# Reordering batch 0's attention in a one-core linear-attention and MLP kernel: part of q loaded behind v, one slot of k rotated on GpSimd

## The chip, the cores and the metric

The kernel runs on one core of a Trainium2 chip. The metric is device time in microseconds (us). The kernel before took 292.59 us (median of 3 runs, 292.51 to 292.88); lower is better. A core has a matrix engine (TensorE, PE in the profile), a vector engine (VectorE, DVE), an activation engine (ScalarE, ACT), GpSimd (POOL) and SyncE (SP), which here only issues DMAs. GpSimd issues DMAs too, among them those that cast from f32 to bf16 on the way.

## What is computed

```python
# q, k, v: [8 batches, 8 heads, 576, 64] f32; w_in [512, 2048], w_out [2048, 512]
theta = pi / 2 * arange(576) / 576
phi(x) = concat([relu(x) * cos(theta), relu(x) * sin(theta)], -1)   # 128 features
kv  = einsum('bhsf,bhsd->bhfd', phi(k), v)
z   = phi(k).sum(axis=2)
num = einsum('bhsf,bhfd->bhsd', phi(q), kv)
den = einsum('bhsf,bhf->bhs', phi(q), z)[..., None] + 1e-06
x   = (num / den) as [4608 tokens, 512]
h   = x @ w_in
out = (h * sigmoid(1.702 * h)) @ w_out
```

## The kernel before

Per batch, 512 of the 576 tokens are worked on at once; the other 64 tokens of each batch (the "tails") are collected in `xt` and go through the MLP together at the end. The program is written as straight-line code, and each engine executes its instructions in the order in which the kernel calls them; buffers come from rotating pools, so an instruction that takes a buffer also waits until the buffer's last reader is done. `pmm` has four PSUM buffers (one bank each), `pat` two (named `at` in the profile, two banks each).

Of batch 0, q, k and v are laid out in nine slots `j` of 64 elements per partition; a tile's half of the partitions is one of two heads. The steps, by name:

- `trig` (L135) makes the features of one slot of q or k: two operations (with cos and with sin), on VectorE, on ScalarE (`act=True`) or on GpSimd (`eng=`). For k they land in `kr`, for q in `qn0`.
- `ksum(j)` (L214) sums k's features over the slots on PE; `ksum_evac` (L221) puts the sum into column 64 of `kvs` on VectorE.
- `qturn_pe(c)` (L167) transposes slots 2c and 2c+1 of q's features on PE, and `qevac(c)` (L174) copies them out into `qT`, on VectorE or (`act=True`) on ScalarE.
- `kv_mm` (L202) multiplies features and v on PE, `kv_evac` (L210) copies the result into `kvs` on VectorE, for heads 0 to 3 and 4 to 7 separately in batch 0.
- `den_early(0)` (L241) computes the denominators of the first 128 tokens ahead of the numerators.
- `num_mm(c)` (L226) makes numerators (and denominators) of 128 tokens in an `at` buffer, `num_div(c)` (L248) divides them on VectorE into `xn`.
- `xturn_mm(c)` (L269) transposes `xn` on PE into the same `at` buffer, and `xturn_evac` (L276) copies it into `x` on ScalarE. `xturn_dma` (L282) does both with one transposing DMA on SyncE; the tail takes it.
- `mm1_part(b, fc, t0, t1)` (L291) is the first MLP matmul for one of the 16 column groups `fc` of w_in and some tokens; `mm1(b, fc)` (L303) does all 512 tokens and `gelu(fc)` (L298) on ScalarE. `mm2` (L327) is the second matmul, and at its end evicts on ScalarE and stores.
- `idle(n, w)` (L341) issues n matmuls on a constant tile, which compute nothing that is used.

Loads of batch 0: SyncE issues k in two DMAs (384 and 768 KB) and q in two (512 and 640 KB, L61 to L63). GpSimd waits for k's first part (a one-element copy, L130) and then issues v in two halves (L132, cast to bf16) and w_in pieces 0 and 1 (L133, L134); after its rotation of q's slot 8, it waits for v (L411) and issues w_in 2 and 3, batch 1's k, q and v, and w_out.

The order around the change is written out by hand from L383 on. Batch 0's attention ends in `start_block(0)` (L354), which interleaves `mm1` of the first four column groups, 128 tokens at a time, with the last numerators and x's transposes, and ends with `mm1(0, 4)`; the loop at L447 goes on with `mm1(0, 5)`. Batch 1 calls the same function with `opened=True`, as it does the opening steps itself. Stores of the last batch go through SyncE, those of the other batches through GpSimd (L338). At the program's end SyncE waits once for each of the semaphores that its DMAs use in turn (eight of them) and for the other queues'.

Of the kernel before, what the change touches and what calls it, by code (L numbers as in the profile page):

```python
# [19 lines left out]
def kernel(  # L20
# [9 lines left out]
    nc = tc.nc  # L30
# [24 lines left out]
    def src_of(src, b, i0=0, i1=NI):  # L55
        return src[b, 2 * i0:2 * i1].rearrange("(i hh) (p j) d -> (hh p) i (j d)", hh=2, j=NS)
# [1 line left out]
    qf = one.tile([128, 2560], F32, name="qf")  # L58
    kf, vf, vb = raw("kf"), raw("vf"), raw("vb", BF16)
    qf0 = qf[:, 0:NI * S].rearrange("p (i e) -> p i e", i=NI)  # L60
    for t, src, cut in ((kf, k, 192), (qf0, q, 256)):  # L61
        nc.sync.dma_start(out=t[:, :, 0:cut], in_=src_of(src, 0)[:, :, 0:cut])  # L62
        nc.sync.dma_start(out=t[:, :, cut:S], in_=src_of(src, 0)[:, :, cut:S])  # L63


    NP = NS + 5
# [56 lines left out]
    def load_win(g):  # L123
        nc.gpsimd.dma_start(out=w_in_sb[g], in_=win_r[:, :, ts(g, 512)])
# [5 lines left out]
    nc.gpsimd.tensor_copy(gate[0:1, 0:1], kf[0:1, 0, 0:1])  # L130
    for i in (0, 2):
        nc.gpsimd.dma_start(out=vb[:, i:i + 2], in_=src_of(v, 0, i, i + 2))  # L132
    load_win(0)  # L133
    load_win(1)  # L134
    def trig(dst, src, j, act=False, eng=nc.vector):  # L135
        i = src[:, :, ts(j, 64)]
        for cs, w in enumerate((cosw, sinw)):
            o = dst[:, j, :, ts(cs, 64)]
            if act:
                nc.scalar.activation(o, i, AF.Relu, scale=w[:, j:j + 1])  # L140
            else:
                eng.tensor_scalar(o, i, 0.0, w[:, j:j + 1], op0=MAX, op1=MUL)  # L142
# [24 lines left out]
    def qturn_pe(c, home=None):  # L167
        tp = pmm.tile([128, 2, NI, 128], BF16, name="mm") if home is None else home
        for j in range(2 * c, min(2 * c + 2, NS)):
            for i in range(NI):  # L170
                nc.tensor.transpose(tp[:, j % 2, i], qn0[:, j, i, :], ident)  # L171
        tps[c] = tp

    def qevac(c, act=False):  # L174
        n = min(2 * c + 2, NS) - 2 * c
        o = qT[:, :, ds(c * 128, n * 64)].rearrange("f h (j p) -> f j h p", j=n)
        i = tps.pop(c)[:, 0:n].rearrange("f j i (hh p) -> f j (i hh) p", hh=2)
        if act:
            nc.scalar.activation(o, i, AF.Copy)
        else:  # L180
            nc.vector.tensor_copy(o, i)

    def at_homes():
        t = pat.tile([128, 2, 512], F32, name="at")
        return [t[:, u].bitcast(BF16).rearrange("p (j i f) -> p j i f", j=2, i=NI) for u in range(2)]
# [24 lines left out]
    def kv_evac(i0, i1, n=65):  # L210
        o = st["kvs"][:, :, i0:i1, 0:n]
        nc.vector.tensor_copy(o, st["ps", i0].rearrange("p hh (i e) -> p hh i e", e=65)[:, :, :, 0:n])  # L212
# [13 lines left out]
    def num_mm(c):  # L226
        ps = pat.tile([128, 2, 512], F32, name="at")
        for h in range(H):
            i, hh = divmod(h, 2)
            nc.tensor.matmul(ps[:, h // 4, ds((h % 4) * 65, 65)], qT[:, h, ts(c, 128)],  # L230
                             st["kvs"][:, hh, i, 0:65], start=True, stop=True)
        nums[c] = [ps]
# [8 lines left out]
    def den_early(c):  # L241
        d = pmm.tile([128, 2, 4], F32, name="mm")
        for h in range(H):
            nc.tensor.matmul(d[:, h // 4, h % 4:h % 4 + 1], qT[:, h, ts(c, 128)],
                             st["kvs"][:, h % 2, h // 2, 64:65], start=True, stop=True)
        return inv_of(d)

    def num_div(c, inv=None):  # L248
        ps = nums[c][0]
        pv = ps[:, :, 0:260].rearrange("p a (h e) -> p a h e", h=4)  # L250
        if inv is None:
            inv = inv_of(pv[:, :, :, 64])
# [10 lines left out]
    def x_open(b):  # L263
        x[b] = xpool.tile([128, KC, MT], BF16, name="xT")
# [4 lines left out]
    def xturn_mm(c):  # L269
        ps, xn = nums[c]  # L270
        xv = xn.rearrange("p a h e -> p (a h e)")
        for kc in range(KC):
            o = ps[:, kc // 2, ds(264 + (kc % 2) * 64, 64)].bitcast(BF16)
            nc.tensor.transpose(o, xv[:, ts(kc, 128)], ident)  # L274

    def xturn_evac(b, c):  # L276
        ps = nums.pop(c)[0]
        i = ps[:, :, 264:392].bitcast(BF16).rearrange("p a (k t) -> p a k t", k=2)
        o = x_of(b, c).rearrange("p (a k) t -> p a k t", a=2)
        nc.scalar.activation(o, i, AF.Copy)  # L280
# [10 lines left out]
    def mm1_part(b, fc, t0, t1):  # L291
        if t0 == 0:
            hp[fc] = pmm.tile([128, MT], F32, name="mm")
        for kc in range(KC):
            nc.tensor.matmul(hp[fc][:, t0:t1], w_in_of(kc, fc), x[b][:, kc, t0:t1],  # L295
                             start=(kc == 0), stop=(kc == KC - 1))

    def gelu(fc):  # L298
        g = gpool.tile([128, MT], BF16, name="g")
        nc.scalar.activation(g, hp.pop(fc), AF.Gelu_apprx_sigmoid)  # L300
        gT[fc] = g
# [25 lines left out]
    def mm2(b, t, lo, hi, c0=0, c1=d_model):  # L327
        if lo == 0:
            yp[t, c0] = pmm.tile([128, d_model], F32, name="mm")
        for fc in range(lo, hi):  # L330
            w = gT[fc][:, ts(t, 128)] if t < 4 else gl_t[:, fc, ts(t - 4, 128)]
            nc.tensor.matmul(yp[t, c0][:, c0:c1], w, w_out_sb[:, fc, c0:c1],  # L332
                             start=(fc == 0), stop=(fc == FC - 1))
        if hi == FC:
            ysb = ypool.tile([128, d_model], F32, name="ysb")
            nc.scalar.activation(ysb[:, c0:c1], yp[t, c0][:, c0:c1], AF.Identity)  # L336
            for p0, n, dst in rows(b, t):
                eng = nc.sync if b == B - 1 else nc.gpsimd  # L338
                eng.dma_start(out=dst[:, c0:c1], in_=ysb[p0:p0 + n, c0:c1])  # L339

    def idle(n, w=None):  # L341
        if w is None:
            w = pmm.tile([128, 512], F32, name="mm")
        for _ in range(n):
            nc.tensor.matmul(w, warm[:, 0:128], warm, start=True, stop=True)  # L345
        return w
# [4 lines left out]
    def vt_rhs(r, i, j):  # L351
        return vt[r, j, i, 0:65]

    def start_block(b, opened=False):  # L354

        if not opened:
            xturn_mm(0)
            xturn_evac(b, 0)
            num_mm(2)
            num_div(2)  # L360
            xturn_mm(1)
            xturn_evac(b, 1)
        def part(c, *fcs):
            for fc in fcs:
                mm1_part(b, fc, c * 128, c * 128 + 128)

        for c in range(2):
            part(c, 0, 1, 2, 3)
            num_mm(c + 3)
            num_div(c + 3)  # L370
            xturn_mm(c + 2)
            xturn_evac(b, c + 2)
        xturn_dma(b, 4)
        part(2, 0, 1, 2)
        part(3, 0, 1)
        part(2, 3)
        part(3, 2, 3)
        for fc in range(4):
            gelu(fc)
        mm1(b, 4)  # L380
# [2 lines left out]
    w = idle(12)  # L383
    for j in (0, 1):
        trig(kr, kf, j)
    for j in (2, 6, 7, 8):
        trig(kr, kf, j, act=True)
    for j in (3, 4, 5):
        trig(kr, kf, j)
    kv_open(0, 2)  # L390
    kv_open(2, 4)
    for j in (0, 1, 2):
        ksum(j)
    for j in (3, 6, 4, 7, 5):
        idle(1, w)
        ksum(j)
    idle(1, w)
    ksum(8)
    for j in (0, 1):
        trig(qn0, qf0, j)  # L400
    ksum_evac()
    idle(1, w)
    qturn_pe(0)
    for j in (2, 3):
        trig(qn0, qf0, j, act=True)
    idle(2, w)
    qturn_pe(1)
    for j in (4, 5):
        trig(qn0, qf0, j)
    trig(qn0, qf0, 8, eng=nc.gpsimd)  # L410
    nc.gpsimd.tensor_copy(gate[0:1, 1:2], vb[0:1, 3, 0:1])  # L411
    load_win(2)
    load_win(3)
    kv_mm(0, 2, vb_rhs, 0, 64)
    qturn_pe(2)
    for j in (6, 7):
        trig(qn0, qf0, j, act=True)
    qevac(0)
    qevac(1)
    qevac(2, act=True)  # L420
    inv0 = den_early(0)
    kv_evac(0, 2, 64)
    kv_mm(2, 4, vb_rhs, 0, 64)
    kv_evac(2, 4, 64)
    qturn_pe(3)
    qevac(3, act=True)
    num_mm(0)
    num_div(0, inv0)
    num_mm(1)
    num_div(1)  # L430
    qturn_pe(4)
    qevac(4)
    idle(2)
    x_open(0)
    start_block(0)


    load(kf, k, 1)
# [57 lines left out]
    num_mm(2)  # L496
    num_div(2)
    mm2(0, 3, 12, 16)
    start_block(1, opened=True)


    for b in range(1, B):
# [73 lines left out]
```

## Time and profile before

| what | us |
|---|---|
| median of 3 runs | 292.59 |
| the profiled execution | 292.54 |
| its span, from the first to the last instruction | 290.8 |
| PE busy | 284.3 (98%) |
| VectorE busy | 124.0 (43%) |
| ScalarE busy | 132.9 (46%) |
| GpSimd busy | 35.9 (12%) |
| mean DMA rate | 180 GB/s |

The page gives for each engine its busy time, then the chain of work that ended last, followed back from the last instruction, with the share of the span of each engine. A timeline row has the start in us, the duration, the engine, the line and the operation, output and inputs with their shapes, and, in brackets, how long the engine had been idle before it and what released it. A group's row has busy time and mean duration in ns. PE's matmuls are pipelined: a 128-column matmul takes 0.22 us, but the next can begin 0.0555 us later. "PEld" is the load of weights ahead of a matmul.

### The profile page before, as it was taken

The numbers are of one execution on the slowest core, as the hardware profiler recorded it, in microseconds if no ns is written. First come the engines' busy times: TensorE is split into PE (matmuls) and PEld (weight loads), VectorE is DVE, ScalarE is ACT, GpSimd is POOL, SyncE is SP. The second block draws the span as 40 slices with busy tenths as digits, with TensorE's granted clock in tenths as the row PEclk, the third lists the DMA queues.
The fourth block names the chain that finished last, engine by engine and source line by source line (L and its number), as shares of the span: only waits on it lengthen the run. The fifth ranks groups of instructions, "written<-read, shape, count | busy, mean of one in ns | idle before, by whom it ended". The sixth has DMA issues, their size and how long they took to land.

```text
span 290.8 us, 5790 instructions
## 1 busy us (share of the span) xinstructions
PE 284.3 (98%) x2331; PEld 155.1 (53%) x2331; DVE 124.0 (43%) x356; ACT 132.9 (46%) x232; POOL 35.9 (12%) x68
## 2 busy tenths in 40 slices
PE   6999999999999999999999999999999999999995
PEld 2785466755555555555455545554555455544444
DVE  4964544933648363826482568156725200000000
ACT  7957654692156214630463136412651167651111
POOL 6650044101210001001100110011000100000000
PEclk9999999999999999999999999999999999999999
DMA  7999999683679858975798479846974400002322
GB/s 250 244 212 290 371 287 367 165 192 104 134 242 288 209 137 292 244 191 145 247 269 218 129 196 319 219 108 182 359 84 79 112 36 3 0 0 57 85 77 72
DMA packets 67866, 52.48 MB, mean 180 GB/s; under 512 B 47968, under 2 KB 57952, under 8 KB 67840
## 3 DMA queue, kind: packets, MB, share of 16 engines
q1 hardware_dynamic: 60560, 32.91, 46.0%
q0 software_dynamic: 7280, 19.21, 22.9%
q8 instruction: 18, 0.29, 0.4%
q14 instruction: 8, 0.07, 0.1%
HBM read 36.70 MB, written 9.44 MB: 159 GB/s over the span
## 4 chain that ended last, share of the span: by engine, by line
PE 96%; DMA 2%; ACT 0%; DVE 0%; SPq 0%; issue 0%; ACTq 0%
PE mm L332 43%; PE mm L295 38%; PE mm L312 5%; PE at L230 3%; PE at L207 3%; DMA kf<-in_k_dram 2%; PE mm L171 1%; PE mm L345 1%; PE at L171 1%; PE at L274 1%; DVE kr L142 0%; PE mm L218 0%; ACT xT L280 0%; SPq L62 0%; ACT ysb L336 0%
## 5 line engine op out<-in xcount | busy, mean ns | idle before, releaser
L332 PE MATMUL mm<-w_out_sb,g 128*128 128x512 bf16 (+1 forms) x528 | 117.9, 373 | 0.0
L295 PE MATMUL mm<-xT,w_in 128*128 128x512 bf16 (+1 forms) x608 | 113.2, 345 | 0.0
L300 ACT ACTIVATE g<-mm 128x512 bf16<-128x512 f32 x128 | 75.2, 599 | 30.2 <-PE mm L295 30.0
L295 PEld LDWEIGHTS <-w_in 128*128 128x128 bf16 x608 | 61.8, 113 | 49.5
L332 PEld LDWEIGHTS <-g 128*128 128x128 bf16 x528 | 48.7, 98 | 49.5
L336 ACT ACTIVATE ysb<-mm 128x512 f32<-128x512 f32 (+1 forms) x37 | 21.7, 586 | 109.7 <-PE mm L332 106.7
L339 POOL DMA_DIRECT2D out_dram<-ysb x36 | 19.4, 540 | 172.9 <-ACT ysb L336 171.1
L142 DVE TENSOR_SCALAR kr<-kf,cosw 128x256 bf16<-128x256 f32 x64 | 22.8, 357 | 30.7 <-DMA kf<-in_k_dram 30.7
L254 DVE TENSOR_TENSOR xn<-at,inv 128x512 bf16<-128x512 f32 x40 | 27.6, 691 | 1.7 <-PE at L230 0.4
L142 DVE TENSOR_SCALAR kr<-kf,sinw 128x256 bf16<-128x256 f32 x64 | 22.1, 345 | 0.0
L236 DVE TENSOR_SCALAR den<-at 128x8 f32<-128x8 f32 x39 | 6.5, 166 | 33.1 <-PE at L230 33.1
L230 PEld LDWEIGHTS <-qT 128*128 128x128 bf16 x320 | 14.6, 97 | 8.1 <-issue 0.8
L212 DVE CAST kvs<-at 128x520 bf16<-128x520 f32 (+1 forms) x9 | 5.6, 635 | 29.6 <-PE at L207 29.6
L230 PE MATMUL at<-kvs,qT 128*128 128x65 bf16 x320 | 15.9, 193 | 0.7 <-ACT xT L280 0.7
L155 DVE TENSOR_SCALAR qn<-qf,sinw 128x512 bf16<-128x512 f32 (+1 forms) x30 | 14.4, 479 | 0.0
L155 DVE TENSOR_SCALAR qn<-qf,cosw 128x512 bf16<-128x512 f32 (+1 forms) x30 | 14.3, 476 | 0.0
L312 PE MATMUL mm<-xt,w_in 128*128 128x512 bf16 x64 | 14.0, 379 | 0.0
L332 PE MATMUL mm<-w_out_sb,gl_t 128*128 128x512 bf16 x64 | 14.0, 379 | 0.0
L313 ACT ACTIVATE gl_t<-mm 128x512 bf16<-128x512 f32 x16 | 9.6, 597 | 4.2 <-PE mm L312 4.2
L312 PEld LDWEIGHTS <-w_in 128*128 128x128 bf16 x64 | 7.2, 113 | 6.6
L207 PEld LDWEIGHTS <-kr 64*128 64x128 bf16 x576 | 9.3, 94 | 2.7 <-issue 2.5
L332 PEld LDWEIGHTS <-gl_t 128*128 128x128 bf16 x64 | 6.2, 98 | 7.6
(63 smaller groups left out, 115.9 us busy)
## 6 DMA issues: line engine op xcount, KB each, us to landing
kf<-in_k_dram SPq DMA_DIRECT2D x5, 1152.0 KB, 6.8
vf<-in_v_dram SPq DMA_DIRECT2D x5, 1152.0 KB, 9.6
qf<-in_q_dram SPq DMA_DIRECT2D x5, 1024.0 KB, 6.0
out_dram<-ysb POOLq DMA_DIRECT2D x20, 256.0 KB, 2.7
kf<-in_k_dram POOLq DMA_DIRECT2D x2, 1152.0 KB, 11.3
vf<-in_v_dram POOLq DMA_DIRECT2D x2, 1152.0 KB, 16.4
w_in<-in_moe_w_in_dram POOLq DMA_DIRECT2D x4, 512.0 KB, 9.3
w_out_sb<-in_moe_w_out_dram POOLq DMA_DIRECT2D x4, 512.0 KB, 18.7
```

What stands on the lines that cost most here:

```text
L142: eng.tensor_scalar(o, i, 0.0, w[:, j:j + 1], op0=MAX, op1=MUL)
L155: nc.vector.tensor_scalar(o, i, 0.0, sc, op0=MAX, op1=MUL)
L207: nc.tensor.matmul(st["kv", i][:, hh, ds(col, n)], kr[r, j, i, :], rhs(r, i, j), start=(j == 0), stop=(j == NS - 1))
L230: nc.tensor.matmul(ps[:, h // 4, ds((h % 4) * 65, 65)], qT[:, h, ts(c, 128)], st["kvs"][:, hh, i, 0:65], start=True, stop=True)
L254: nc.vector.tensor_tensor(xn, pv[:, :, :, 0:64], inv.unsqueeze(3).to_broadcast([128, 2, 4, 64]), op=MUL)
L295: nc.tensor.matmul(hp[fc][:, t0:t1], w_in_of(kc, fc), x[b][:, kc, t0:t1], start=(kc == 0), stop=(kc == KC - 1))
L300: nc.scalar.activation(g, hp.pop(fc), AF.Gelu_apprx_sigmoid)
L312: nc.tensor.matmul(hps, w_in_of(kc, fc), xt[:, kc, :], start=(kc == 0), stop=(kc == KC - 1))
L313: nc.scalar.activation(gl_t[:, fc, :], hps, AF.Gelu_apprx_sigmoid)
L332: nc.tensor.matmul(yp[t, c0][:, c0:c1], w, w_out_sb[:, fc, c0:c1], start=(fc == 0), stop=(fc == FC - 1))
L336: nc.scalar.activation(ysb[:, c0:c1], yp[t, c0][:, c0:c1], AF.Identity)
L339: eng.dma_start(out=dst[:, c0:c1], in_=ysb[p0:p0 + n, c0:c1])
```

## The change

Loads: q's slots 0 to 5 come in one DMA from SyncE behind k, and slots 6 to 8 in one DMA from GpSimd behind v. The four w_in pieces are issued together on GpSimd, behind the rotation of k's slot 8, which moves there from ScalarE; the wait of L411 is gone.

Order: batch 0's steps are interleaved anew. q's slot 4 moves to ScalarE and slots 6 and 7 are rotated later there; the eviction of `qturn_pe(1)` goes from VectorE to ScalarE and that of `qturn_pe(2)` from ScalarE to VectorE; `qturn_pe(3)` is put behind `xturn_mm(0)`, and `qturn_pe(4)`, `num_mm(4)` and the tail's DMA around `mm1(0, 4)`. Of the fillers, three stand ahead of `ksum(8)` instead of one, and five others are gone. `start_block` is left to batch 1, where it turns and evicts x's last 128 tokens ahead of `num_mm(4)` instead of behind it. In the last batch the two stores of the first tail tile go through GpSimd instead of SyncE.

```diff
-    for t, src, cut in ((kf, k, 192), (qf0, q, 256)):
-        nc.sync.dma_start(out=t[:, :, 0:cut], in_=src_of(src, 0)[:, :, 0:cut])
-        nc.sync.dma_start(out=t[:, :, cut:S], in_=src_of(src, 0)[:, :, cut:S])
+    for t, src, c0, c1 in ((kf, k, 0, 192), (kf, k, 192, S), (qf0, q, 0, 384)):
+        nc.sync.dma_start(out=t[:, :, c0:c1], in_=src_of(src, 0)[:, :, c0:c1])
...
     for i in (0, 2):
         nc.gpsimd.dma_start(out=vb[:, i:i + 2], in_=src_of(v, 0, i, i + 2))
-    load_win(0)
-    load_win(1)
+    nc.gpsimd.dma_start(out=qf0[:, :, 384:S], in_=src_of(q, 0)[:, :, 384:S])
...
-                eng = nc.sync if b == B - 1 else nc.gpsimd
+                last = b == B - 1 and t != 4
+                eng = nc.sync if last else nc.gpsimd
...
-    def start_block(b, opened=False):
...
-        for c in range(2):
-            part(c, 0, 1, 2, 3)
-            num_mm(c + 3)
-            num_div(c + 3)
-            xturn_mm(c + 2)
-            xturn_evac(b, c + 2)
+    def start_block(b):
+        part(b, 0, 0, 1, 2, 3)
+        num_mm(3)
+        num_div(3)
+        xturn_mm(2)
+        xturn_evac(b, 2)
+        part(b, 1, 0, 1, 2, 3)
+        xturn_mm(3)
+        xturn_evac(b, 3)
+        num_mm(4)
+        num_div(4)
         xturn_dma(b, 4)
...
-    for j in (2, 6, 7, 8):
+    for j in (2, 6, 7):
         trig(kr, kf, j, act=True)
     for j in (3, 4, 5):
         trig(kr, kf, j)
+    trig(kr, kf, 8, eng=nc.gpsimd)
+    for g in range(4):
+        load_win(g)
...
-    idle(1, w)
+    idle(3, w)
     ksum(8)
     for j in (0, 1):
         trig(qn0, qf0, j)
     ksum_evac()
-    idle(1, w)
     qturn_pe(0)
-    for j in (2, 3):
+    for j in (2, 3, 4):
         trig(qn0, qf0, j, act=True)
-    idle(2, w)
     qturn_pe(1)
-    for j in (4, 5):
-        trig(qn0, qf0, j)
-    trig(qn0, qf0, 8, eng=nc.gpsimd)
-    nc.gpsimd.tensor_copy(gate[0:1, 1:2], vb[0:1, 3, 0:1])
-    load_win(2)
-    load_win(3)
+    qevac(0)
+    trig(qn0, qf0, 5)
     kv_mm(0, 2, vb_rhs, 0, 64)
-    qturn_pe(2)
-    for j in (6, 7):
-        trig(qn0, qf0, j, act=True)
-    qevac(0)
-    qevac(1)
-    qevac(2, act=True)
     inv0 = den_early(0)
+    qevac(1, act=True)
     kv_evac(0, 2, 64)
     kv_mm(2, 4, vb_rhs, 0, 64)
     kv_evac(2, 4, 64)
-    qturn_pe(3)
-    qevac(3, act=True)
+    qturn_pe(2)
+    trig(qn0, qf0, 8, eng=nc.gpsimd)
+    for j in (7, 6):
+        trig(qn0, qf0, j, act=True)
     num_mm(0)
     num_div(0, inv0)
     num_mm(1)
+    qevac(2)
     num_div(1)
-    qturn_pe(4)
-    qevac(4)
-    idle(2)
     x_open(0)
-    start_block(0)
+    xturn_mm(0)
+    xturn_evac(0, 0)
+    qturn_pe(3)
+    qevac(3, act=True)
+    num_mm(2)
+    num_div(2)
+    part(0, 0, 0, 1)
+    xturn_mm(1)
+    xturn_evac(0, 1)
+    part(0, 0, 2, 3)
+    num_mm(3)
+    num_div(3)
+    xturn_mm(2)
+    xturn_evac(0, 2)
+    part(0, 1, 0, 1, 2, 3)
+    part(0, 2, 0)
+    xturn_mm(3)
+    xturn_evac(0, 3)
+    part(0, 2, 1, 2, 3)
+    part(0, 3, 0, 1, 2, 3)
+    for fc in range(4):
+        gelu(fc)
+    qturn_pe(4, at_homes()[0])
+    qevac(4)
+    mm1(0, 4)
+    num_mm(4)
+    num_div(4)
+    xturn_dma(0, 4)
```

Here `part(b, c, *fcs)` calls `mm1_part` for 128 tokens `c` and the column groups `fcs`.

More of the change, by code (lines that the diff above doesn't have):

```diff
@@ L352, in vt_rhs, with part @@
         return vt[r, j, i, 0:65]
-    def start_block(b, opened=False):
[L356 to L365, printed above, removed]
-        for c in range(2):
-            part(c, 0, 1, 2, 3)
-            num_mm(c + 3)
-            num_div(c + 3)
-            xturn_mm(c + 2)
-            xturn_evac(b, c + 2)
+    def part(b, c, *fcs):
+        for fc in fcs:
+            mm1_part(b, fc, c * 128, c * 128 + 128)
+    def start_block(b):
[9 more added lines that the diff above has]
+        num_div(4)
         xturn_dma(b, 4)
[L374 to L377, printed above, removed]
+        part(b, 2, 0, 1, 2)
+        part(b, 3, 0, 1)
+        part(b, 2, 3)
+        part(b, 3, 2, 3)
         for fc in range(4):
@@ L429 @@
     num_mm(1)
+    qevac(2)
     num_div(1)
-    qturn_pe(4)
+    x_open(0)
+    xturn_mm(0)
[21 more added lines that the diff above has]
+    qturn_pe(4, at_homes()[0])
     qevac(4)
-    idle(2)
-    x_open(0)
-    start_block(0)
+    mm1(0, 4)
+    num_mm(4)
+    num_div(4)
+    xturn_dma(0, 4)
     load(kf, k, 1)
@@ L498 @@
     mm2(0, 3, 12, 16)
-    start_block(1, opened=True)
+    start_block(1)
     for b in range(1, B):
```

## The prediction

> **What bounds the kernel.** I read the page's chain of work first, then the busy time by stage, the same chain between 4 and 22 us, the timeline of all engines up to 25 us and the end of SyncE's row.
>
> ```profile
> PE 96%; DMA 2%; ACT 0%; DVE 0%; SPq 0%; issue 0%; ACTq 0%
> ```
>
> TensorE is the chain. The stages show where it is not full (columns: stretch, its length, then PE's busy time and the other engines'):
>
> ```profile
> 4.00:16.00 12.00, 10.37 (x201) 7.33 (x200) 10.23 (x30) 9.26 (x20) 9.41 (x14) 1.00 1.17 278
> 16.00:21.61 5.61, 5.59 (x96) 5.08 (x94) 3.19 (x9) 3.35 (x7) 2.35 (x4) 1.00 1.25 211
> 21.61:287.30 265.69, 265.57 (x2033) 141.60 (x2031) 109.67 (x310) 116.75 (x202) 22.62 (x40) 1.00 0.67 178
> 287.30:290.80 3.50, 0.00 (x0) 0.00 (x0) 0.00 (x0) 0.38 (x1) 0.00 (x0) 1.00 0.11 37
> ```
>
> From 21.61 to 287.30 PE is busy 265.57 of 265.69 us. So a change of batch 0 is worth exactly the shift of the instant at which `mm1(0, 5)` can begin (21.61 us before), and beyond that only the 3.5 us behind PE can give. Batch 0's chain joins PE's dense run here (start, length, what):
>
> ```profile
> 14.89 0.02 issue
> 14.91 0.60 ACT xT L280
> 15.52 0.04 issue
> 15.56 0.40 PE at L230 x8
> 15.96 0.22 PE at L274 x4
> 16.18 0.89 PE mm L295 x16
> ```
>
> From 15.56 PE never stands: 64 `mm1` matmuls of 128 columns (0.0555 us apart, 3.55 us), three `num_mm` and three turns of x (1.6 us with their hand-overs) reach `mm1(0, 4)` at 20.75, which takes 0.86. Ahead of 15.56 are fillers and waits. Can the new order start sooner and stay dense?
>
> **1. The loads.** All four w_in pieces and v share one stream: k's second part (768 KB) landed at 6.24, q's first 512 KB at 7.65, v's halves at 10.73 and 12.15, w_in 0 and 1 at 14.75 and 17.83. At the 386 to 395 GB/s that the stretches from 3 to 8 us show, 384 KB of q moved behind v are worth 1.0 us: q's first six slots land at about 8.3 (768 KB behind k), v at 9.7 and 11.15, q's rest at 12.15. **w_in 0 stays at 14.75**, since the bytes ahead of it are the same. In `mm1` nothing can begin before; that is the floor. The other end: v's first packet came 4.1 us after its issue (at 8.47), while SyncE's loads were still being served. If that is a fixed delay and not the queue ahead, v does not move up with the bytes, and the stream stands idle: v at 10.3 and 11.75, q's rest at 12.85, w_in 0 at 15.4. I take the first, because GpSimd's later stores, with little in the queue, had their first packet 1.1 us after issue. w_in is now issued after the rotation of k (9.15 to 12.3 instead of 5.99); with 1.1 us it is there before the stream, at 12.15, needs it. Batch 1's k is issued on GpSimd at about 14.6 (13.87 before) and reached by the stream at 23, so that costs nothing; of w_out the tightest piece landed at 39.57 and was used at 39.96, and with the late stream (40.2) PE comes as late (40.3).
>
> **2. k's slot 8 on GpSimd.** It costs two of these (the two POOL rows), and leaves ScalarE 0.8 us earlier:
>
> ```profile
> 9.88 1.20 POOL L142 TENSOR_SCALAR qn<-qf,cosw 128x256 bf16<-128x256 f32 x1 [2.37 <-DMA qf<-in_q_dram]
> 9.97 0.66 PEld L171 LDWEIGHTS <-qn 128*128 128x128 bf16 x8
> 9.99 0.57 DVE L142 TENSOR_SCALAR qn<-qf,sinw 128x256 bf16<-128x256 f32 x1
> ...
> 10.48 0.34 DVE L142 TENSOR_SCALAR qn<-qf,cosw 128x256 bf16<-128x256 f32 x1
> ...
> 11.09 1.14 POOL L142 TENSOR_SCALAR qn<-qf,sinw 128x256 bf16<-128x256 f32 x1
> ```
>
> GpSimd is free at 6.77 (its third issue then ends), so k's slot 8 is done at 6.80 + 2.34 = 9.15. PE meets `ksum(8)` behind `ksum(5)` (0.22 later than before, see below) and three fillers of 0.213, at 9.42; so 0.25 us are to spare. Behind `ksum(8)` on PE stand all of q's turns, and on VectorE `ksum_evac`: from about 9.7 on, each us that GpSimd is late is a us on everything.
>
> The reader should see the price to VectorE too: its operation took 0.57 beside GpSimd's start and 0.34 wholly inside GpSimd's 1.20 us. The same 0.2 us were lost at 4.81, 6.26 and 7.07, beside GpSimd's load issues. I charge 0.2 once for each further GpSimd instruction that meets a rotation on VectorE: k's slot 5 ends at 8.63 (8.41 before), q's slot 1 and slot 5 lose 0.2 each.
>
> The Trainium skill, "SBUF — State Buffer", section "Who interferes with whom", speaks against this edit: of a VectorE operation in a two-port mode and a GpSimd one, "Whoever issues first gets the shared pair for the whole instruction; the other **fully blocks** (not throttle)." The operation at 10.48 disagrees, as it ran inside GpSimd's; what the rule would give is the slower rival below.
>
> **3. VectorE's chain** (steps at the rows' pitch: rotation 0.265, q's eviction 0.59, kv's 0.30, division 0.69; 0.04 to 0.05 for each hand-over). Rotations of q 0 and 1 end at 9.88, `ksum_evac` at 9.99; `qturn_pe(0)` ends at 10.32; first eviction of q 10.35 to 11.02, **0.8 earlier** than 11.15 to 11.82. Slot 5 to 11.75, `inv0` to 12.06, kv's evictions to 12.66 (13.36 before; their matmuls start at 10.60 and 11.42, behind v). First division 13.03 to 13.72, **0.70 earlier**. Now comes what was put in between: the eviction of `qturn_pe(2)`, formerly ScalarE's, takes 0.6 on VectorE, so the second division is 14.66 to 15.35, only **0.11 earlier** than 14.77 to 15.46.
>
> **4. PE's run.** `xturn_mm(0)` at 13.76, its eviction 14.18 to 14.77 (ScalarE rotates q's slots 7 and 6 from 12.18 to 13.87, just in time), `qturn_pe(3)` and `num_mm(2)` beside it, first `mm1` part at 15.06 instead of 16.02. What PE has left from there: 64 matmuls of 0.0555 (3.55), three turns and `qturn_pe(4)` (0.89), two `num_mm` (0.49), `mm1(0, 4)` (0.86): 5.8 us. And three waits: `num_mm(3)` takes the second of the two `at` buffers, which the eviction of `xturn_mm(1)` frees at 16.51, behind `qevac(3)` (1.02) on ScalarE: 0.39. `part(3)` waits 0.17 for the last x, `xturn_mm(3)` 0.03. Sum 15.06 + 5.79 + 0.59 = 21.44. The same walk over the kernel before ends at 21.48 where the trace has 21.61, so 0.13 goes on top: 21.57. **Front: -0.05 us.** The early start is spent: `qturn_pe(3)`, `qturn_pe(4)` and the waits now lie inside the run that was dense before. Bounds: without the collisions VectorE is 0.3 earlier and w_in 0 is the floor, -0.31; with the late stream +0.34. The fillers taken out leave PE gaps of at most 0.4 us; after gaps of 0.95 and 0.69 (at 7.20 and 15.56) its granted clock stayed at 1.00, so I charge nothing.
>
> **5. Block 1** gets `start_block`'s new order too. Before, `num_mm(4)` (0.24) filled the time until the third division ended at 52.16, and later PE stood 0.18 at 53.29 for the last x. Now it stands 0.27 at once for that division, and not later: +0.06.
>
> **6. The stores.** Two tails' issues go to GpSimd, which is idle at 263 us, at nothing (cover gone: 0.54 each). The first tail's transposing DMA leaves SyncE at about 22.8 instead of 19.91; the next on that queue came at 53.5 and `mm1_tails` at 245, so it too is free. But one SyncE load and two stores fewer move the last store by three of the eight semaphores that SyncE's DMAs use in turn, from number 2 to number 7. At the end SyncE asks for them in the order 0 to 7:
>
> ```profile
> L571 SPq EVENT_SEMAPHORE  x6: 27/28/28, 289.6 to 289.9; - x6
> ```
>
> These six are the one for the last store (landed 289.62) and five behind it, 0.06 us apart. In the changed program's order the last store's is the last asked for, and the others pass while it is in flight: **-0.30 us**. If they did not, 0.
>
> **Sum.** The profiled execution took 292.54 (span 290.8 and 1.7 around it), the median is 292.59: 292.54 - 0.05 + 0.06 - 0.30 = 292.25.
>
> **Rivals.** A measurement tells about 0.2%, 0.58 us, from no change: below 292.0 is faster, above 293.2 slower.
> - *Forecast, 0.60*: the gain in front is given back; 291.95 to 292.65 with the late stream.
> - *VectorE runs free, 0.20*: no further collisions, and w_in 0, the floor, up to 0.3 early; front -0.3 to -0.6, so 291.7 to 292.0. For it: stores issued on GpSimd later (108.9 us) cost VectorE nothing. Against: every load issue in front did.
> - *w_in comes late, 0.08*: 4.1 us after the issue at 9.15 as v did, so the stream stands from 12.15 to 13.3 and w_in 0 lands at 15.9: front +0.8, 293.05. Against: nothing of SyncE's is queued then.
> - *GpSimd stands behind VectorE, 0.09, slower*: k's slot 8 starts only when VectorE's run over k ends (8.41), is done at 10.75, and `ksum(8)` holds PE, `ksum_evac` and the first eviction of q by 1.1 us: 293.4. It decides from 9.7 us on. For it: VectorE's six operations are back to back there; against: GpSimd started at 9.88 amid four of them.
> - *The end does not shorten, 0.03*: 292.55.
>
> **Range** 291.7 to 293.0: the third rival and both bounds of the loads are nearly in it, the fourth is left out. Faster 0.21 (the second, and the first's low end), within 0.2% 0.70, slower 0.09.
>
> **What would show it.** Right: q's first eviction near 10.4, first division near 13.0 but the second near 14.7; first `mm1` part near 15.1; a wait of PE for ScalarE's xT of 0.3 to 0.4 near 16.5; `mm1(0, 5)` near 21.5; one SyncE wait behind the last landing. Wrong: k's slot 8 ending past 9.7 us, w_in 0 landing past 15.2, or `mm1(0, 5)` before 21.2.

## The result, and the profile after

The changed kernel took 293.55 us (median of 10 runs, 293.07 to 294.29) beside 292.69 for the kernel before (median of 10): a ratio of 1.0028, 95% interval 1.0019 to 1.0037. It is slower, and outside the range of 291.7 to 293.0. The profiled execution took 293.35 us (span 291.65), 0.81 more than that of before.

The stages of the changed kernel, cut at the first `mm1` part, at `mm1(0, 5)` and behind PE's last matmul (stretch, its length, then PE's busy time and the other engines'):

```profile
4.00:15.81 11.81, 10.59 (x190) 6.73 (x189) 10.10 (x27) 8.74 (x20) 10.66 (x13) 1.00 1.14 273
15.81:22.79 6.98, 6.37 (x107) 5.58 (x103) 2.75 (x8) 4.31 (x8) 4.10 (x7) 1.00 1.23 230
22.79:288.50 265.71, 265.50 (x2038) 141.51 (x2034) 110.58 (x313) 116.51 (x201) 24.30 (x42) 1.00 0.67 177
```

PE is still full from `mm1(0, 5)` on, so the time is again the shift of that instant and the end: 22.79 instead of 21.61 is +1.18; from there to the start of PE's last matmul it took 265.35 (265.34 before); and from that start to the end of the span 3.50 instead of 3.88, -0.38. The sum is +0.81. The whole loss arises ahead of 22.79 us, where the forecast had 21.57.

The chain of waits of the changed kernel in that stretch (start, length, what):

```profile
6.20 2.91 DVE kr L140 x6
9.11 1.35 DVE qn L140 x4
10.46 0.04 issue
10.51 0.84 PE mm L169 x12
11.35 0.64 PE at L205 x36
...
13.75 0.70 DVE xn L252
...
17.34 0.37 PE at L228 x7
17.71 0.36 issue
18.07 0.19 PE at L228
```

Two things are to be seen. The chain runs through VectorE's rotations of k, which last 2.91 us for six (2.15 before, 6.26 to 8.41), and reaches the first division at 13.75: the forecast had 13.03, the kernel before 13.73. And in the middle of `num_mm(3)`, between its seventh and its eighth matmul, PE stands 0.36 us for "issue", that is for nothing that the profile shows as a releaser. From start to start the eighth matmul comes 0.55 behind the seventh instead of 0.03, so all that follows is 0.52 later.

VectorE's and GpSimd's rows of the changed kernel, in its timeline, show why k took so long:

```profile
6.90 1.19 POOL L140 TENSOR_SCALAR kr<-kf,cosw 128x256 bf16<-128x256 f32 x1
6.95 0.75 DVE L140 TENSOR_SCALAR kr<-kf,cosw 128x256 bf16<-128x256 f32 x1
7.63 0.62 DVE L140 TENSOR_SCALAR kr<-kf,sinw 128x256 bf16<-128x256 f32 x1
8.04 1.30 POOL L140 TENSOR_SCALAR kr<-kf,sinw 128x256 bf16<-128x256 f32 x1
8.17 0.68 DVE L140 TENSOR_SCALAR kr<-kf,cosw 128x256 bf16<-128x256 f32 x1
8.77 0.33 DVE L140 TENSOR_SCALAR kr<-kf,sinw 128x256 bf16<-128x256 f32 x1
```

Of the four VectorE operations that start inside one of GpSimd's, three take 0.62 to 0.75 us instead of 0.34; the fourth, at 8.77, takes 0.33.

The loads are late too. Of v's two DMAs in the changed kernel (issue, then issue to landing):

```profile
L131 POOL DMA_DIRECT2D vb<-in_v_dram x2: 763/842/922, 4.4 to 5.4; - x2
DMA to landing us min/median/max: 6.2/6.5/6.7
```

That is 10.64 and 12.07 us, 0.09 and 0.08 earlier than before for 384 KB fewer ahead of it; the forecast had 9.7 and 11.15. q's first six slots landed at 8.77 (forecast 8.3), its last three at 13.06 (12.15), w_in 0 at 15.66 (14.75). Neither v (12.07) nor w_in 0 is what the chain above waits for, but the second product with v starts at 12.21, only 0.14 behind its landing.

The stores did what was said. SyncE's waits of the changed kernel at the end, from 289.0 us on and then from 290.5 on:

```profile
L585 SPq EVENT_SEMAPHORE  x9: 27/28/28, 289.3 to 290.7; - x9
...
L585 SPq EVENT_SEMAPHORE  x1: 28/28/28, 290.7 to 290.7; - x1
```

The last landing is at 290.73, and one wait stands behind it instead of six.

### The profile page after: what moved, and what is told of

Its sections match the earlier page's. It is cut to its first block, busy times and chain, and to the rows that moved or that the text cites. A ratio compares the mean times of both kernels' runs of the same rounds, so it can differ in the third digit from the quotient of the medians.

```text
span 291.6 us, 5781 instructions
## 1 busy us (share of the span) xinstructions
PE 285.2 (98%) x2328; PEld 154.9 (53%) x2328; DVE 124.4 (43%) x354; ACT 133.1 (46%) x232; POOL 40.6 (14%) x72
## 4 chain that ended last, share of the span: by engine, by line
PE 94%; DVE 2%; DMA 2%; ACT 1%; issue 0%; SPq 0%; ACTq 0%
PE mm L330 43%; PE mm L293 38%; PE mm L310 5%; PE at L228 3%; PE at L205 3%; DMA kf<-in_k_dram 2%; DVE kr L140 1%; PE at L169 1%; PE at L272 1%; DVE xn L252 0%; PE mm L169 0%; DVE qn L140 0%; ACT xT L278 0%; SPq L62 0%; ACT ysb L334 0%
## 5 line engine op out<-in xcount | busy, mean ns | idle before, releaser
L338 POOL DMA_DIRECT2D out_dram<-ysb x38 | 20.7, 547 | 203.1 <-ACT ysb L334 202.7
L140 DVE TENSOR_SCALAR kr<-kf,sinw 128x256 bf16<-128x256 f32 x64 | 22.7, 355 | 0.0
```

## The experiments

All times in one table. The runs were made on different chips; each ratio is to runs of the kernel before made beside it, whose medians lie between 292.51 and 292.69, so 0.2 us between the medians of two rows says nothing. "k" is the end of VectorE's rotations of k, "v" v's two landings, "division" the start of the first division; `mm1(0, 5)` is, where its first record is missing, the start of `mm1(0, 4)` plus 1.10 (new order) or 0.86 (old), as the complete records show. Landings and starts are those of the profiled execution.

| kernel | median us | ratio to before, 95% | k | v | division | first mm1 | mm1(0, 5) |
|---|---|---|---|---|---|---|---|
| before | 292.69 | | 8.41 | 10.73, 12.15 | 13.73 | 16.02 | 21.61 |
| after | 293.55 | 1.0028 (1.0019 to 1.0037) | 9.11 | 10.64, 12.07 | 13.75 | 15.81 | 22.79 |
| e1 small fillers | 293.14 | 1.0031 (1.0014 to 1.0049) | 9.09 | 10.46, 11.92 | 13.73 | 15.80 | 22.27 |
| e2 k's slot 8 on ScalarE | 293.13 | 1.0024 (1.0009 to 1.0040) | 8.34 | 11.77, 13.19 | 14.77 | 16.84 | 23.28 |
| e3 q on SyncE | 292.79 | 1.0003 (0.9995 to 1.0012) | 8.42 | 10.80, 12.20 | 13.79 | 15.85 | 22.30 |
| e4 both | 293.39 | 1.0026 (1.0013 to 1.0039) | 8.55 | 11.22, 12.62 | 14.20 | 16.27 | 22.71 |
| e5 before, stores | 292.12 | 0.9982 (0.9973 to 0.9990) | 8.27 | 10.69, 12.10 | 13.69 | 15.98 | 21.56 |
| e7 v issued early | 293.68 | 1.0033 (1.0020 to 1.0047) | 8.37 | 9.72, 11.10 | 14.53 | 16.60 | 23.04 |
| e8 q's turn earlier | 293.22 | 1.0024 (1.0013 to 1.0035) | 8.41 | 10.62, 12.00 | 13.62 | 16.34 | 22.78 |
| e9 before, k on GpSimd | 292.57 | 0.9999 (0.9989 to 1.0009) | 8.48 | 11.21, 12.58 | 14.18 | 16.47 | 22.05 |
| e10 q late on SyncE | 294.20 | 1.0048 (1.0020 to 1.0076) | 8.44 | 10.43, 11.89 | 13.47 | 17.16 | 23.60 |
| e11 the same, k on ScalarE | 299.01 | 1.0204 (1.0184 to 1.0224) | 8.70 | 9.66, 11.08 | 13.29 | 21.14 | 28.21 |
| e12 new order, less v | 292.55 | 0.9990 (0.9978 to 1.0003) | 8.45 | 10.06, 10.87 | 13.14 | 15.21 | 21.66 |
| e13 old order, less v | 292.04 | 0.9969 (0.9957 to 0.9981) | 8.50 | 10.22, 11.01 | 13.73 | 16.02 | 21.60 |
| e14 old order, no fillers | 292.15 | 0.9989 (0.9977 to 1.0001) | 8.31 | 10.70, 12.10 | 13.68 | 15.97 | 21.56 |
| e15 the same, less v | 291.93 | 0.9973 (0.9963 to 0.9983) | 8.15 | 9.96, 10.75 | 13.50 | 15.79 | 21.37 |

**The stores alone.** e5 is the kernel before with this edit (a third tail store moves too, so that the last store takes semaphore no. 7):

```diff
-                eng = nc.sync if b == B - 1 else nc.gpsimd
+                last = b == B - 1 and t != 4 and not (t == 5 and p0 == 0)
+                eng = nc.sync if last else nc.gpsimd
```

> The kernel before with the last batch's first three tail stores on GpSimd, nothing else: the last store then has the last of the eight semaphores, as in the changed kernel. By the prediction's step 6 one SyncE wait follows the last landing instead of six, five times 0.06 us: 0.30 us faster, 292.4 beside 292.7. The rival: the end is the last landing and the barrier whatever the order, no difference.

It took 292.12 us against 292.51 of its own runs of before, and in its profile too one SyncE wait stands behind the last landing. So the stores are worth about 0.4 us (0.3 to 0.8 by the ratio's interval), and everything else in the change cost 1.25 (profiled executions, 293.35 against 292.10).

**The pause in `num_mm(3)`.** The fillers at the start of PE's program are made 48 of 128 columns instead of 12 of 512, so that PE's instructions are fetched at other times against its work; nothing else is changed.

```diff
-    w = idle(12)
+    w = pmm.tile([128, 512], F32, name="mm")
+    for _ in range(48):
+        nc.tensor.matmul(w[:, 0:128], warm[:, 0:128], warm[:, 0:128], start=True, stop=True)
```

> The changed kernel with its first twelve fillers of 512 columns cut into forty-eight of 128 columns: the same time on the array, 36 matmuls and weight loads more ahead of all work. The pause of 0.36 us of PE in the middle of num_mm(3) (17.71 to 18.07, the profile names no cause) comes while a 16 KB packet of the instruction queue, begun at 15.83, is under way; before, such a packet began at 14.35 and PE stood from 14.88 to 15.56 anyway. Theory code: PE ran out of instructions; with 36 more ahead the fetch comes over 1 us earlier in the work, the pause goes, and the time falls by 0.3 to 0.5, to about 293.1. Theories GpSimd and loads: the pause belongs to the operands or to the loads, it stays, and the time stays at 293.5.

The front is the same as in the changed kernel until 17.3 us (first division 13.73, first part 15.80), but `num_mm(3)` runs through. The timeline of e1:

```profile
17.34 0.40 PE L228 MATMUL at<-kvs,qT 128*128 128x65 bf16 x8 [0.24 <-ACT xT L278]
17.58 0.39 PE L272 MATMUL at<-ident,xn 128*128 128x128 bf16 x4
```

`mm1(0, 4)` starts 0.51 earlier than in the changed kernel (21.17 against 21.68), and the profiled execution takes 0.49 less (292.86 against 293.35). The medians don't show the gain: beside its own runs of before e1 is 0.63 slower and the changed kernel 0.86, and their ratios can't be told apart. In the records, a packet of 16 KB on the instruction queue begins at 15.83 in the changed kernel, 2.2 us ahead of the eighth matmul of `num_mm(3)`; in e1 it begins at 11.34. In before it came at 14.35 and ran while PE stood anyway for `xT` (14.88 to 15.56). In r1 and r2, two more executions of the changed kernel (below), the pause is at the same matmul (0.21 and 0.32). Here and in these two that matmul, 0.03 behind the seventh, would have come 1.7 to 2.0 us behind the start of the packet, and started 2.2 to 2.5 behind it. In e2, e3, e4, e7 and e8, with the fillers unchanged, it comes 2.6 to 3.2 us behind such a start, and PE does not stand. This fits PE running out of instructions: the new order has the place where it runs out in its dense run, with a few tenths of a microsecond deciding. The records do not name the engine that a packet is for; that it is PE's is argued from these times.

**GpSimd beside VectorE, and q's queue.** e2 puts k's slot 8 back on ScalarE; e3 puts q's last slots back on SyncE; e4 does both; e9 puts k's slot 8 on GpSimd in the old order of e5, with w_in 0 and 1 issued behind it.

```diff
# e2
-    for j in (2, 6, 7):
+    for j in (2, 6, 7, 8):
         trig(kr, kf, j, act=True)
...
-    trig(kr, kf, 8, eng=nc.gpsimd)
# e3
-    for t, src, c0, c1 in ((kf, k, 0, 192), (kf, k, 192, S), (qf0, q, 0, 384)):
+    for t, src, c0, c1 in ((kf, k, 0, 192), (kf, k, 192, S), (qf0, q, 0, 384),
+                           (qf0, q, 384, S)):
...
-    nc.gpsimd.dma_start(out=qf0[:, :, 384:S], in_=src_of(q, 0)[:, :, 384:S])
```

> The changed kernel with k's slot 8 rotated on ScalarE again; all else as changed, so w_in is issued on GpSimd from 6.9 on instead of 9.31. Theory GpSimd: VectorE's rotations of k no longer stretch (0.57 to 0.75 us each in the changed kernel, 0.34 alone), k's slot 5 ends at 8.4 to 8.6 instead of 9.11, q's slots 0 and 1 at about 9.7 instead of 10.45; the gain is 0.5 or more, 293.0. Theory loads: v still lands at 10.6 and 12.1 and holds the second kv matmuls at 12.2, so the first division stays near 13.7 and the gain is at most 0.15 unless w_in 0 lands earlier than 15.66.

> The changed kernel with q's slots 6 to 8 loaded by SyncE behind its slots 0 to 5, ahead of v, as before; one more tail store goes to GpSimd so that the last store keeps its place among the semaphores. Theory loads: q's rest lands near 9.8 instead of 13.06, ScalarE's rotation of slots 7 and 6 and GpSimd's of slot 8 no longer stand behind it, and w_in 0 lands near 14.8 to 15.2; v stays at 10.7 and 12.1 since it did not move up in the changed kernel either; gain 0.3 or more, 293.2. Theory GpSimd: VectorE is as stretched as in the changed kernel, first division near 13.7, gain under 0.15.

> Both moves of the front are undone (k's slot 8 on ScalarE, q's last slots on SyncE behind its first six); the new order and the stores stay (a third tail store goes to GpSimd too, so that the last store keeps its semaphore). Theory (the new order itself costs time, about 0.6 us behind the kernel before with the same stores, which took 292.12; GpSimd's rotation is covered, since v lands last): 292.7 to 293.0 as e3 (292.79), first mm1 near 15.9, mm1(0, 5) near 22.5. Rival (GpSimd's rotation of k and the load on its queue are the price of the change): both are gone, so 292.1 to 292.3 and mm1(0, 5) at 21.6 to 21.9.

> The kernel before with three tail stores on GpSimd, as in e5 (292.12), and with k's slot 8 rotated on GpSimd ahead of the issues of w_in 0 and 1; nothing else is changed. Theory (v lands last, and covers what GpSimd's rotation and its collisions with VectorE cost): k's rotations on VectorE end within 0.5 us of 8.3, v's products start with v's landing, and the time is 292.0 to 292.4. Rival (the rotation on GpSimd costs on the path): ksum(8) or the first eviction of q is 0.5 or more later, mm1(0, 5) with it, 292.6 to 293.2.

In e2 VectorE's rotations of k end at 8.34, so the stretch comes from GpSimd's rotation and not from its DMA issues. (Its profiled execution, 294.17, is a late one beside the median of 293.13: v landed at 13.19 and binds.) But e3 keeps that rotation, and they end at 8.42. The timeline of e3:

```profile
6.34 1.19 POOL L140 TENSOR_SCALAR kr<-kf,cosw 128x256 bf16<-128x256 f32 x1 [0.25 <-DMA kf<-in_k_dram]
6.45 0.57 DVE L140 TENSOR_SCALAR kr<-kf,sinw 128x256 bf16<-128x256 f32 x1
6.93 0.34 DVE L140 TENSOR_SCALAR kr<-kf,cosw 128x256 bf16<-128x256 f32 x1
7.20 0.49 DVE L140 TENSOR_SCALAR kr<-kf,sinw 128x256 bf16<-128x256 f32 x1
```

The same work on both engines, begun 0.56 us earlier on GpSimd since it has no third load to issue: the operations beside its first one take 0.57, 0.34 and 0.49, and VectorE's six take 2.25 us instead of 2.91. This goes through all kernels that rotate k on GpSimd: where that starts at 6.28 to 6.40 (e3, e7, e8, e9, e10), VectorE's k ends at 8.37 to 8.48; where it starts at 6.79 to 6.94, behind the third issue (the changed kernel three times, e1), at 9.01 to 9.15. What in the phase decides it isn't settled.

Yet e3's first division is at 13.79, no earlier. The chain of e3, ahead of the second product with v:

```profile
5.33 6.87 DMA vb<-in_v_dram
12.20 0.04 issue
12.24 0.71 PE at L205 x36
```

With VectorE free, v binds at the same instant (12.24; 12.21 in the changed kernel). The two stand in parallel, so undoing one shows nothing in front. What e3 gains in its profiled execution, 0.46 us (292.89 against 293.35), is the pause, which it does not have: from the first part to `mm1(0, 5)` it takes 6.45 instead of 6.98. e4 should have been as fast as e3 and was 0.6 slower: v landed at 12.62 and binds, and PE stood 0.26 up to 43.28 for an eviction of batch 1's q. e9 was 0.45 slower than e5, not 0.0 to 0.3: v landed at 12.58, and its late first product (11.26) waits in its chain for v's first landing (11.21), not for the rotation. r3 below shows such landings without any rotation on GpSimd, so the price of the rotation in the old order stays open between 0 and 0.45.

**An earlier v, and one step of the order.** e7 drops the copy that holds GpSimd until k's first part is there, so v is issued at 2.3 us; e8 is e3 with `qturn_pe(3)` and its eviction ahead of `xturn_mm(0)`.

```diff
# e7
-    nc.gpsimd.tensor_copy(gate[0:1, 0:1], kf[0:1, 0, 0:1])
# e8
-    xturn_mm(0)
-    xturn_evac(0, 0)
     qturn_pe(3)
     qevac(3, act=True)
+    xturn_mm(0)
+    xturn_evac(0, 0)
```

> The changed kernel without the one-element copy that holds v's issue on GpSimd until k's first part has landed: v is issued at about 2.3 us instead of 4.4. Theory (v's landing is set by the queues ahead of it and by the engines that it finds busy, not by the bytes that SyncE has left): v's first packets come 1 to 2 us earlier and v lands at 9.0 to 10.2 and 10.5 to 11.7; the first division then starts at 13.1 to 13.4 instead of 13.75, and the time is 292.9 to 293.2. Rival (the bytes share one stream): k and q land later by what v gains, 0.5 to 1.5 us, VectorE's rotations follow them, and the time is 293.4 to 294.0.

> e3 (q's last slots on SyncE) with one step of the order moved: the transpose of q's slots 6 and 7 and its eviction on ScalarE come ahead of the first transpose of x instead of behind it. Theory (ScalarE's eviction of q, 1.02 us ahead of the second eviction of x, holds num_mm(3) and every later part): the second eviction of x ends 0.3 to 0.6 earlier than 17.32, mm1(0, 5) starts 0.2 to 0.4 earlier than 22.52, 292.4 to 292.6. Rival (the eviction only changes its place on ScalarE, and the first x comes later by as much): first mm1 at 16.2 to 16.8, time 292.8 to 293.3.

In e7 v lands at 9.72 and 11.10, as its theory had it, but q's first slots at 9.54 (8.77 in the changed kernel); the chain goes through them, and the division comes at 14.53. For the time (293.68) that is the rival: the bytes share one stream. e8 is its rival too: the first x is 0.5 later (first `mm1` part 16.34), and nothing comes back.

**Why v landed late.** e10 issues q's last slots on SyncE behind q's first ones' landing, so nothing of q stands behind v in GpSimd's queue, and has the small fillers; e11 also takes GpSimd's rotation of k away. r1 and r2 are the changed kernel again, r3 and r4 are e5 again, each one execution.

```diff
-    nc.gpsimd.dma_start(out=qf0[:, :, 384:S], in_=src_of(q, 0)[:, :, 384:S])
...
+    nc.scalar.activation(qf0[0:1, 0, 384:385], qf0[0:1, 0, 0:1], AF.Copy)
+    nc.sync.dma_start(out=qf0[:, :, 384:S], in_=src_of(q, 0)[:, :, 384:S])
```

> The changed kernel with two things taken away: q's last slots leave GpSimd's queue (SyncE issues them when q's first six slots have landed, near 8.8 us, so that v still has the stream first), and the instruction fetch pause (the 12 fillers of 512 columns are 48 of 128, as in e1). A third tail store goes through GpSimd, so that the last store keeps its semaphore. Theory (v's bytes did move up, but one late DMA engine holds each landing, and such engines come with a second load behind v in GpSimd's queue): v's last packet ends near 10.9 and v lands at 9.7 to 10.0 and 11.2 to 11.4; first division 13.1 to 13.6, mm1(0, 5) at 21.6 to 22.0, time 292.2 to 292.6, with a narrow spread of the runs. Rival (late engines come whatever queue follows): v lands after 10.4 and 11.7, time 292.9 to 293.3.

> e10 with k's slot 8 on ScalarE again, so GpSimd rotates nothing beside VectorE. Theory (with v early, VectorE's collisions with GpSimd, 1.0 us up to q's slot 1, are the next thing on the path): k's rotations end near 8.4, first eviction of q near 10.4, first division 0.2 to 0.4 before e10's, time 0.2 to 0.4 below e10's. Rival (v still binds): the same time as e10 within 0.2.

> The changed kernel once more, for a second look at its loads. Theory (with q's last slots behind v in GpSimd's queue, one DMA engine of the sixteen is late in most executions): the middle packet of v ends near 9.2, its last later than 11.4, v lands at 10.3 to 10.8 and 11.7 to 12.2. Rival (the late engine of the first profile was chance): the last packet ends before 11.0, v lands at 9.7 and 11.1, and the execution takes 292.6 to 293.0.

> The same again: by the theory v's last packet ends later than 11.4, by the rival before 11.0.

> The kernel before with three tail stores on GpSimd, once more, where w_in stands behind v in GpSimd's queue. Theory (a late engine goes with q's last slots behind v): v's last packet ends at 11.7 to 11.9, 0.5 or less behind its 95th hundredth. Rival (a late engine comes as often here): in one of two looks the last packet ends 0.6 or more behind it.

> The same again: by the theory no late engine, by the rival one in one of the two.

As an experiment on time e10 and e11 failed: q's last slots, now beside w_in, landed at 14.66 and 18.07, and ScalarE, PE and the rest waited for them (294.20, with runs from 292.99 to 299.17, and 299.01). For v, e10 went to its rival (10.43 and 11.89). e11 has the early landing:

```profile
L131 POOL DMA_DIRECT2D vb<-in_v_dram x2: 761/840/919, 4.4 to 5.3; - x2
DMA to landing us min/median/max: 5.3/5.5/5.8
```

That is 9.66 and 11.08, the forecast's 9.7 and 11.15. The packets of v (512 in each kernel) say what differs; ends in us:

```
           first starts   half   95%    last    lands
before         8.47      10.16  11.44  11.86    12.15
after          7.50       9.22  10.61  11.72    12.07
r1 (after)     7.48       9.33  10.92  12.00    12.34
r2 (after)     7.43       9.32  10.69  11.52    11.86
e1             7.44       9.19  10.53  11.53    11.92
e2             7.39       9.45  11.35  12.86    13.19
e10            7.46       9.18  10.47  11.56    11.89
e11            7.38       9.08  10.37  10.75    11.08
r3 (e5)        8.60      10.39  11.76  12.28    12.63
```

In the changed kernel v did move up with the bytes, by 0.97 at its first packet, 0.94 at the half and 0.83 at 95%. But its last packets come in single file, 0.09 us apart, which I take for one engine's (the records name no engine), and v's landing, 0.35 behind the last packet, moved by 0.08. The Trainium skill, "DMA: Bandwidth & Descriptors", section "Why a DMA increments its semaphore by 16 and not by 1", says that a DMA runs on up to 16 engines that finish independently and that the semaphore counts each of them; the rows fit that: 95% of v's packets were there 1.46 us before the landing.

In five of the six profiles of kernels with q's last slots behind v on GpSimd (after, r1, r2, e1, e2) the last packet is 0.83 to 1.51 us behind the 95%. The sixth is e7, where v is issued 2 us earlier: it has 0.24, and v, q's last slots and w_in 0 landed there at 11.10, 12.04 and 14.56, the forecast's 11.15, 12.15 and 14.75. In ten profiles of the others with all of v the distance is 0.25 to 0.80 (0.53 in r3, between its theory and its rival, 0.25 in r4), and 1.09 in e10. So a late engine came more often with the changed queue, but neither always nor only with it. In the five, the longest single packet of v took 0.48 (after) to 1.32 us (e2) instead of 0.107; but e3, e4, e10 and r3 have packets of 0.42 to 0.71 too, and what makes an engine late stays open. The changed kernel took 293.40 and 293.34 in r1 and r2, with v at 12.34 and 11.86; in r2, as in the first profile, VectorE's late k is on the chain, in r1 v. e5 took 292.68 and 292.44 in r3 and r4, beside one execution of before at 292.65, so these two do not confirm its gain: in r3 v came at 12.63, and in r4 PE stood 0.23 for w_in 0, which landed at 16.21. In both the end is as short as in e5, 3.51 us from the start of PE's last matmul.

**v early for certain.** e12 has the new order with k's slot 8 on ScalarE, q on SyncE and the small fillers; e13 is e5. In both, v's DMAs load only five of the nine slots, so part of v is left out:

```diff
+    nc.vector.memset(vb[:, :, 320:S], 0.0)
...
-        nc.gpsimd.dma_start(out=vb[:, i:i + 2], in_=src_of(v, 0, i, i + 2))
+        nc.gpsimd.dma_start(out=vb[:, i:i + 2, 0:320], in_=src_of(v, 0, i, i + 2)[:, :, 0:320])
```

> The new order with k's slot 8 on ScalarE, q's last slots on SyncE, small fillers and three tail stores on GpSimd, and only five of the nine slots of batch 0's v loaded (the others are set to zero), so v and w_in land early whatever the queue does: it leaves part of v out, for its time alone. Theory (the new order, behind an early v, reaches mm1(0, 5) where the forecast put it, and no earlier): v at 9.6 to 10.2 and 10.8 to 11.2, first division 12.9 to 13.4, mm1(0, 5) at 21.4 to 21.8, time 291.8 to 292.3. Rival (the order is slow for another reason than v): first division after 13.5 or mm1(0, 5) after 22.1, time above 292.6.

> The order of before with three tail stores on GpSimd (e5, 292.12) and the same cut of v (five of nine slots loaded, the others zero; part of v left out). Theory (the old order has less between v and mm1(0, 5), and gains from an early v as well until VectorE's rotations and evictions of q bind): first division 13.0 to 13.4, mm1(0, 5) 21.1 to 21.5, time 291.5 to 291.9, below e12's. Rival (the new order is the better one as soon as v is early): 292.0 or more here and e12 below it.

The chain of e12 at the first division and at PE's wait for x:

```profile
13.14 0.70 DVE xn L253
...
16.09 0.61 ACT xT L279
16.69 0.04 issue
16.73 0.40 PE at L229 x8
```

With v at 10.87 and VectorE's k at 8.45, the new order does what the forecast's steps 3 and 4 say: first division 13.14 (13.03), first part 15.21 (15.06), a wait for ScalarE's x that costs 0.40 from start to start, up to 16.73 (0.39 up to 16.51), `mm1(0, 5)` 21.66 (21.57). So even then it is no earlier than the old order (21.61 before, 21.60 in e13): the gain in front is given back. e12's time of 292.55, 0.25 above the range that I expected, has one more stall, 0.24 up to 42.21, where PE waits for ScalarE's eviction of batch 1's q.

e13 did not gain from its early v at all, against my theory, and its chain has PE's fillers on it. So:

```diff
     ksum_evac()
-    idle(1, w)
     qturn_pe(0)
...
-    idle(2, w)
     qturn_pe(1)
...
     qevac(4)
-    idle(2)
     x_open(0)
```

> The order of before with three tail stores on GpSimd (e5) and without the five fillers that stand behind ksum(8), ahead of the second transpose of q and ahead of the first transpose of x. In e5 the chain of PE's own work (transposes of q and fillers) reaches the first product with v at 10.78, 0.09 behind v's landing, and the last two fillers hold the first transpose of x by 0.13. Theory (v binds next): 0.1 to 0.25 are gained, mm1(0, 5) at 21.3 to 21.5, time 291.85 to 292.05. Rival (gaps of PE cost clock, or PE's fetch pauses come back): 292.1 or more.

> The same without the five fillers, and with five of the nine slots of batch 0's v loaded (the others zero; part of v left out), as in e13 (292.04). Theory (in e13 the early v was wasted because PE's fillers and VectorE's evictions of q came later than v): the first product with v starts at 10.2 to 10.5 instead of 10.81, first division 13.2 to 13.5 instead of 13.73, time 291.5 to 291.8. Rival (VectorE's evictions of q bind, fillers or not): first division at 13.6 to 13.7, 291.9 to 292.0.

Nothing is gained with v as it is (e14, the rival's 292.1 or more). With less of v, e15's time is the rival's (291.93) and its first division the theory's (13.50): `mm1(0, 5)` is 0.23 earlier than in e13 (21.37 against 21.60), but the ratios (0.9973 and 0.9969) don't tell the two apart. The chain of e14 tells what stood beside the fillers all the time:

```profile
6.28 2.50 ACT kr L140 x6
8.78 1.60 ACT qn L140 x4
10.38 0.05 issue
10.43 0.40 PE mm L171 x4
10.82 0.64 PE at L207 x36
```

ScalarE's ten operations, from k's landing on, end 0.3 before v lands. In the old order three chains (ScalarE, PE with its fillers, v) reach the first product with v within about 0.1 us (10.73 in e5, 10.76 in e14; v landed at 10.69 and 10.70), so no single one of them is worth more than that; with v early too, e15 starts it at 10.59. Of the versions that load all of v, e5, the stores alone, has the lowest time; e14 isn't told apart from it.

## Why the prediction was wrong

- **Step 1 failed in part.** "I take the first": v at 9.7 and 11.15. v's bytes came as early as that, its landing didn't (10.64 and 12.07), because the last packets, one engine's by their spacing, were a microsecond late; what made them late is open. The other end that I had given (10.3 and 11.75) rests on another mechanism, a fixed delay of 4.1 us, and is refuted by the first packet at 7.50, 3.1 us after its issue. w_in 0 landed at 15.66, past my bound of 15.4 and just ahead of the first part (15.81); the forecast's 15.06 could not have been met behind it either.
- **Step 2 was mis-sized, and it is the step on the chain of the profiled execution.** "I charge 0.2 once for each further GpSimd instruction that meets a rotation on VectorE": 0.22 by k's end; measured 0.70 (9.11 against 8.41), and 0.99 by q's slot 1 (10.45 against 9.46; forecast 0.42). The 0.2 was what single VectorE operations had lost beside GpSimd in the trace of before; three in a row that lose 0.3 to 0.4 each, as here, it did not show. The Trainium skill's rule that I quoted, "SBUF — State Buffer", section "Who interferes with whom", by which the later one is fully blocked, is not what the rows show either: the operation at 6.95, 0.05 behind GpSimd's, ended at 7.70, 0.39 before it. k's slot 8 itself was done at 9.34, before my bound of 9.7; the fourth rival's 293.4 is near the result by chance: in it GpSimd waits for VectorE and ends at 10.75, which did not happen.
- **Steps 3 and 4** were right in their working and wrong in their input: from the first part to `mm1(0, 5)` I had 6.51, e12 has 6.45, e3 6.45, and the changed kernel 6.98, with the pause in it, a term that step 4 had at nothing. The first part came 0.75 late (15.81 for 15.06), the pause put 0.52 on top, and the rest of the run took 0.05 less than I had: these are the 1.22 between 21.57 and 22.79. Each of the two late inputs, v and VectorE's k, is enough for the 0.75, as the chains of r2 (VectorE) and e3 (v) show.
- **Step 5**: +0.06 forecast; the whole stretch from `mm1(0, 5)` to PE's last matmul took 0.01 more.
- **Step 6** was right: -0.30 forecast, one wait behind the landing, -0.38 in the changed kernel's end, and a ratio of 0.9982 for the stores alone.
- **The range**: its upper end, 293.0, has room for a first part that is 0.75 late (292.25 + 0.75), whichever input makes it late, and for nothing on top. The pause went past it.

## What to carry to other kernels

A load has landed when its slowest DMA engine is done: bytes taken off the queue move the bulk, not surely the landing, so a step that waits for a landing is costed from the last packet. When several chains meet within a few tenths of a microsecond, an order made for an earlier input pays its moved work in full and gets the gain only if all of them move. A transfer's or a collision's price read from one encounter needs the spread of all encounters as its bound.

## What was not expected of the hardware

- PE stood 0.32 to 0.36 us (0.21 in r1) in the dense run, as it seems for its own instructions, and went on 2.2 to 2.5 us behind the start of a 16 KB instruction packet. The kernels e1 to e15 show 0.16 of such "issue" twice later on, about 25 us apart (up to 43.63 and 68.36 in e12). e5 shows it too, but its two further executions r3 and r4, on another chip, don't, so it isn't the kernel's alone.
- GpSimd's two rotations (1.15 to 1.30 us each) beside VectorE's six operations went with 2.25 us for the six (e3) or 2.91 (the changed kernel), where before they took 2.15; the two cases differ in which engine began when.
- 384 KB on SyncE's queue, issued at about 8.9 us while w_in was in GpSimd's, took 9.2 us to land (e11); queued ahead of v, the same load landed at 9.37 (e3).
